# Giving VectorE 64 of the 1024 exponential units of a fused attention and spectral kernel

## The chip, the cores and the metric

The kernel runs on one core of one Trainium2 chip. The metric is device time in microseconds (us), as a median over runs. Engines of the core are called PE (TensorE: matmuls, with PEld for its weight loads), DVE (VectorE), ACT (ScalarE), POOL (GpSimd) and SP (SyncE, which here only issues DMAs). Each engine takes its own instructions in the order in which the program gives them; between engines they wait for each other by semaphores.

## The reference

Two branches are computed from one input `x` of 2048 tokens by 448 features and are mixed by a gate:

```python
x = A_x
g = _sigmoid((x * gate_w).sum(-1, keepdims=True))
a = _A_ref(x, A_wqkv, A_wo)      # softmax attention
b = _B_ref(x, B_w_r, B_w_i)      # irfft2(rfft2(x) * W)
return g * a + (1 - g) * b
```

In `_A_ref` there are 16 heads of 28 features: `q`, `k`, `v` come from `x @ wqkv`, then `p = softmax(q k^T * 28**-0.5)`, `o = p v`, and the heads together are multiplied by `wo`. The exponentials of the softmax are 16 x 2048 x 2048 values, and they are what the kernel is built around. `_B_ref` is a two-dimensional real Fourier transform, a product with a complex filter, and the transform back; the kernel does it with matmuls against constant matrices. Everything enters and leaves as bf16.

## The kernel before, in words

**Prologue.** `x` is loaded and transposed on PE, and the first keys and queries are projected. From then on the method `stream` (line 463) writes the order of PE, ACT and DVE by hand, in a loop over steps.

**Units and groups.** A group `g` is a block of 512 queries and four heads; there are 16. In a group, the 2048 keys are cut into 16 blocks `i` of 128, and each of the four heads `j` gives one *unit*: scores of 128 keys by 512 queries, which are one PSUM bank. So there are 16 x 16 x 4 = 1024 units. The four units of one `(g, i)` are a *quad*.

**A step.** [...]Five hold scores, as two slots of three and two banks (`SLOTS`), one holds the running product with `v` (`psPV`), and two rotate for everything else (`ps_bg`, line 158: the *background banks*). One step works through one slot. ACT takes the exponential of its two or three banks in one ACTIVATE (line 662) and writes bf16 into a ring of 15 places. PE meanwhile writes the scores of the next step into the other slot (`scores`, line 546, with matmuls on line 549), and multiplies a quad whose four exponentials are ready with `v` (`pv`, line 569; four matmuls on line 577). When a group's 16 quads are in, `finish_group` (line 713) copies `psPV` away and sets two later tasks going, which divide by the row sums.

**Background.** The other work is two generators of small pieces, one for the projections of attention and one for the Fourier branch. A background tile is filled by PE in one of the two banks, in two to four pieces, and emptied by DVE. `background` (line 511) gives PE pieces until their sum reaches `rate` times the index of the current unit, so they are spread evenly over the units; `st["open"]` tells that a tile is half filled. At the end, blocks of the output projection (`out_block`, line 743) join it.

**Filler.** Each step takes `HEAT` = 340 columns per unit of ACT from an account, and each background piece pays its columns in. When the account is negative, one matmul on zeros is put ahead of the scores of the next step (line 564), and 512 is paid in.

**The code that the change switches on.** `pick` (line 634) can take a quad out of the list that ACT works through (`taken`), and put its two halves, of two units each, on a list for DVE. `vscores` (line 612) gives at most one unit's score matmul per step, and only where no background tile is half filled. `vpair` (line 596) takes a background bank for it and lets DVE move the bank to an int32 tile with a clamp and an offset. When both units of the half are there, `vnext` (line 622) gives the pieces of `vexp` (line 756), which forms the exponential from integer and fraction by a polynomial, in six DVE instructions over 1024 elements. The planner gives pieces as long as its count of DVE's work, `self.dv`, is below `st["vtime"]`, which grows by 0.47 for every unit of ACT. With `VQ` = 0 the first line of `pick` always returns, and none of this is in the program.

## Time and profile before

| What | Value |
|---|---|
| Time, median of three runs | 509.69 us (509.38 to 510.75) |
| Profiled execution: its time, and the span from first to last instruction | 510.75 us, 508.9 us |
| Stretch of the exponentials in the span | 23.8 to 489.9 us |
| ACT, PE, DVE busy in that stretch of 466.1 us | 464.63, 430.47, 178.14 us |
| Granted PE clock, mean over the span | 0.983 |

Busy time is the time in which an engine runs at least one instruction that works on data; instructions of one engine can overlap, so that their durations added up are more than that. The ends of matmuls are modelled in the profile. An idle time is put down to the instruction whose semaphore came last.

### The profile page before, as it was taken

To read this page: it belongs to the slowest core of one execution; us is meant where nothing else is said; L and a number is where in the kernel's file an instruction comes from. 1 tells how busy PE (TensorE), PEld (TensorE's weight loads), DVE (VectorE), ACT (ScalarE), POOL (GpSimd) and SP (SyncE) were. 2 spreads that over 40 slices of the span, in tenths; PEclk is the share of its full clock that TensorE was granted. 3 is DMA by queue.
4 is the path that set the end of the run, shared out by engine and by line. 5 is a ranking of instruction groups with operands and counts; after the bars stand their busy time and mean duration, and the time that the engine had idled before them with its cause. 6 is when DMAs were issued, how large, how long until landed. Compare 5 with 4: busy or idle time off the path is not lost.

```text
span 508.9 us, 7848 instructions
## 1 busy us (share of the span) xinstructions
PE 453.6 (89%) x3306; PEld 159.2 (31%) x3333; DVE 195.5 (38%) x355; ACT 473.3 (93%) x426; POOL 13.8 (3%) x43
## 2 busy tenths in 40 slices
PE   6799999999999999899999999999999999998943
PEld 3433222243233333343333332233233323322211
DVE  3622323422344446645664444423344322322202
ACT  2599999999999999999999999999999999999950
POOL 7100000000000000000000000000000000000000
PEclk9999999999999999999999999999999999999986
DMA  7620000001000012312200000001001011001101
GB/s 244 145 56 9 17 7 4 21 1 30 1 23 0 20 27 51 80 44 66 52 23 13 1 22 23 32 12 34 12 20 34 15 48 32 29 27 32 36 4 55
DMA packets 28138, 17.85 MB, mean 35 GB/s; under 512 B 18568, under 2 KB 25160, under 8 KB 28104
## 3 DMA queue, kind: packets, MB, share of 16 engines
q1 hardware_dynamic: 26184, 17.06, 11.9%
q8 instruction: 26, 0.43, 0.3%
q10 hardware_dynamic: 1920, 0.30, 0.3%
q14 instruction: 8, 0.07, 0.0%
HBM read 15.25 MB, written 1.97 MB: 34 GB/s over the span
## 4 chain that ended last, share of the span: by engine, by line
ACT 85%; PE 8%; DMA 3%; DVE 2%; SPq 1%; issue 0%; ACTq 0%; DVEq 0%
ACT ring L662 85%; PE pf L748 3%; PE psS L549 2%; PE psPV L577 1%; DMA wst_65<-in_A_wqkv_dram 1%; DMA rb<-scr_639 1%; DMA wst_66<-in_A_wqkv_dram 1%; PE psS L564 1%; PE xt L319 1%; DMA rs<-oU 0%; PE pk L256 0%; DVE kT_138 L264 0%; DMA scr_639<-rc 0%; DVE kmin L276 0%; SPq L169 0%
## 5 line engine op out<-in xcount | busy, mean ns | idle before, releaser
L662 ACT ACTIVATE ring<-psS 128x1536 bf16<-128x1536 f32 (+1 forms) x410 | 464.7, 1389 | 4.1 <-PE psS L549 3.6
L577 PE MATMUL psPV<-ring,vsb 128*32 128x512 bf16 x1024 | 102.7, 389 | 0.4 <-ACT ring L662 0.3
L564 PE MATMUL psS<-zero 128*128 128x512 bf16 x219 | 82.6, 377 | 15.0 <-ACT ring L662 12.6
L549 PE MATMUL psS<-qT_136,kT_140 32*128 32x512 bf16 x256 | 40.2, 383 | 6.0 <-ACT ring L662 4.6
L549 PE MATMUL psS<-qT_134,kT_138 32*128 32x512 bf16 x256 | 40.2, 383 | 5.8 <-ACT ring L662 3.9
L577 PEld LDWEIGHTS <-vsb 128*32 128x32 bf16 x1024 | 26.5, 92 | 58.5 <-issue 58.4
L549 PE MATMUL psS<-qT_135,kT_139 32*128 32x512 bf16 x256 | 40.2, 383 | 5.0 <-ACT ring L662 3.7
L549 PE MATMUL psS<-qT_137,kT_141 32*128 32x512 bf16 x256 | 40.1, 383 | 2.0 <-ACT ring L662 1.4
L807 DVE CAST U<-psA 128x512 bf16<-128x512 f32 x32 | 22.0, 691 | 22.9 <-PE psA L803 22.9
L549 PEld LDWEIGHTS <-kT_138 32*128 32x128 bf16 x256 | 12.3, 90 | 44.0 <-issue 41.2
L549 PEld LDWEIGHTS <-kT_141 32*128 32x128 bf16 x256 | 11.4, 90 | 42.7 <-issue 41.6
L549 PEld LDWEIGHTS <-kT_140 32*128 32x128 bf16 x256 | 12.6, 90 | 38.6 <-issue 36.6
L564 PEld LDWEIGHTS <-zero 128*128 128x128 bf16 x219 | 21.4, 98 | 8.5 <-issue 7.5
L549 PEld LDWEIGHTS <-kT_139 32*128 32x128 bf16 x256 | 12.7, 90 | 35.0 <-issue 32.6
L407 DVE CAST vsb<-pvx 128x448 bf16<-128x448 f32 x16 | 10.0, 627 | 32.4 <-PE pvx L403 32.4
L886 DVE TENSOR_SCALAR bm_sb<-psY,omg 128x448 bf16<-128x448 f32 x16 | 10.9, 684 | 29.4 <-PE psY L881 29.4
L719 DVE COPY oU<-psPV 128x512 f32<-128x512 f32 x16 | 11.1, 691 | 26.0 <-PE psPV L577 25.8
L881 PE MATMUL psY<-Binv_sb,ZT 128*128 128x448 bf16 x64 | 20.6, 360 | 0.0
L751 DVE SCALAR_TENSOR_TENSOR fin<-pf,gsb,bm_sb 128x448 bf16<-128x448 f32 x16 | 10.9, 684 | 24.2 <-PE pf L748 24.2
L909 DVE CAST ZT<-psZ 128x512 bf16<-128x512 f32 x16 | 11.1, 691 | 15.9 <-PE psZ L905 15.8
L403 PEld LDWEIGHTS <-xT 128*128 128x128 bf16 x256 | 13.7, 97 | 10.9 <-issue 9.5
L748 PE MATMUL pf<-Wo_sb,qT_137 128*128 128x448 bf16 x16 | 6.5, 408 | 9.1 <-DVE qT_137 L735 9.1
(231 smaller groups left out, 425.2 us busy)
## 6 DMA issues: line engine op xcount, KB each, us to landing
RBg<-cRB SPq DMA_DIRECT2D x16, 128.0 KB, 2.8
rb<-scr_638 SPq DMA_DIRECT2D x8, 256.0 KB
rb<-scr_639 SPq DMA_DIRECT2D x8, 256.0 KB
Wg<-in_B_w_r_dram SPq DMA_DIRECT2D x32, 56.2 KB, 1.9
xtok<-in_A_x_dram SPq DMA_DIRECT2D x4, 448.0 KB, 5.7
out_dram<-fin SPq DMA_DIRECT2D x16, 112.0 KB, 1.7
CSg<-cCS SPq DMA_DIRECT2D x16, 96.0 KB, 1.9
Wg<-in_B_w_i_dram SPq DMA_DIRECT2D x16, 56.2 KB, 2.0
```

The source lines that it names most:

```text
L403: nc.tensor.matmul(pv[:, k, 0:N], lhsT=self.xT[:, c, 128 * t:128 * (t + 1)], rhs=w[:, c, 2 * n0:2 * n0 + N], start=(c == 0), stop=(c == se ...
L549: nc.tensor.matmul(ps, lhsT=self.kT[T][r:r + 32, 128 * i:128 * (i + 1)], rhs=self.qT[T][r:r + 32, QW * b:QW * (b + 1)], start=True, stop=T ...
L564: nc.tensor.matmul(psS[:, 0, :], lhsT=self.zero[:, 0:P], rhs=self.zero[:], start=True, stop=True)
L577: nc.tensor.matmul(psPV[g][r:r + 32, :], lhsT=self.vsb[:, i, 4 * T + j, :], rhs=ring[:, p, :] if isinstance(p, int) else p, start=(count[g ...
L662: ex = nc.scalar.activation(out=ring[:, rp:rp + ne, :], in_=psS[:, 0:ne, :], func=ACT.Exp, scale=self.LN)
L719: nc.vector.tensor_copy(out=oU[:], in_=psPV[:])
L748: nc.tensor.matmul(pf[:, 0:D], lhsT=self.oT[T][:, 128 * t:128 * (t + 1)], rhs=self.Wo_sb[:, T, :], start=(T == 0), stop=(T == self.NTL - 1))
L751: nc.vector.scalar_tensor_tensor(out=fin[:], in0=pf[:, 0:D], scalar=self.gsb[:, t:t + 1], in1=self.bm_sb[:, t, :], op0=ALU.mult, op1=ALU.add)
L807: nc.vector.tensor_copy(out=self.U[:, :, :, :, t * J:t * J + J].rearrange("p b r g j -> p (b r g) j"), in_=ps[:].rearrange("p b (r j) -> p ...
L881: nc.tensor.matmul(psY[:, 0:D], lhsT=Z[0:fn, fb, ri, :], rhs=self.Binv_sb[0:fn, qi, :], start=(qi == 0), stop=(qi == nq - 1))
L886: nc.vector.tensor_scalar(out=self.bm_sb[:, g, :], in0=psY[:, 0:D], scalar1=self.omg[:, g:g + 1], scalar2=None, op0=ALU.mult)
L909: nc.vector.tensor_copy(out=Zs[g][:].rearrange("p b r m -> p (b r m)"), in_=psZ[:].rearrange("p b n -> p (b n)"))
```

## The change

One constant is set: how many quads DVE takes.

```diff
@@ class Kernel @@
     RING = 15
     HEAT = 340
-    VQ = 0
+    VQ = 16
     LATE = 6
```

The line that reads it, and the one that decides whether a piece of the DVE's exponential is given now:

```python
if self.VQ * st["units"] <= len(taken) * self.NU:      # in pick; NU is 1024
    return
...
while self.dv < st["vtime"] and vnext():               # in the step
    pass
```

With 16 there is one quad for every 64 units, which is one in each group. It is taken in the first steps of the group (in the first 6 of its 16 key blocks, `LATE`), and it is the group's last key block that is not taken yet. All that follows from it, the steps of ACT, the fillers and the places of the background pieces, is laid out anew by the same planner.

## The prediction
> **What bounds the kernel now.** I read the page's busy shares first, then the windows of the stretch of exponentials, then waits, groups, and the timeline.

> ```profile
> PE 453.6 (89%) x3306; PEld 159.2 (31%) x3333; DVE 195.5 (38%) x355; ACT 473.3 (93%) x426; POOL 13.8 (3%) x43
> ...
> L662 ACT ACTIVATE ring<-psS 128x1536 bf16<-128x1536 f32 (+1 forms) x410 | 464.7, 1389 | 4.1 <-PE psS L549 3.6
> ...
> L564 PE MATMUL psS<-zero 128*128 128x512 bf16 x219 | 82.6, 377 | 15.0 <-ACT ring L662 12.6
> ```

> The exponentials keep ACT busy for 464.7 of the 466.1 us between the first and the last of them. ACT waits 3.6 us in all, 2.7 of it once, at the start. So ACT sets the end: one unit costs 464.7/1024 = 0.454 us, a step 464.7/410 = 1.13 us. Before and after lie 510.75 - 466.1 = 44.7 us (prologue, last output blocks), which the edit does not touch. But PE is close behind, and the same windows show where DVE is loaded (columns: stretch, length, busy time and count of PE, PEld, DVE, ACT, POOL, clock, DMA share, GB/s).

> ```profile
> 53.10:82.20 29.10, 26.80 (x174) 7.70 (x175) 9.97 (x19) 29.10 (x28) 0.74 (x2) 1.00 0.04 11
> ...
> 169.50:198.60 29.10, 26.99 (x206) 9.89 (x205) 14.85 (x29) 29.10 (x27) 0.53 (x1) 1.00 0.13 35
> 198.60:227.70 29.10, 26.86 (x238) 10.99 (x238) 16.38 (x36) 28.96 (x27) 0.00 (x0) 1.00 0.24 60
> 227.70:256.80 29.10, 27.00 (x215) 10.50 (x216) 16.96 (x38) 28.80 (x26) 0.00 (x0) 1.00 0.24 59
> ...
> 373.20:402.30 29.10, 27.29 (x191) 9.00 (x191) 10.48 (x18) 29.10 (x27) 0.00 (x0) 1.00 0.10 28
> ```

> A window is one group of 64 units. PE is busy for about 27 of 29.1 us in every one, DVE for 9 to 17. ACT loses time only where DVE is fullest, and the timeline shows how:

> ```profile
> 215.76 0.62 DVE L858 TENSOR_TENSOR cm_t_2359<-psB,Wg 128x450 bf16<-128x450 f32 x1
> ...
> 216.44 0.37 PE L403 MATMUL pvx<-wst_65,xT 128*128 128x112 bf16 x4 [0.72 <-DVE cm_t_2359 L858]
> ...
> 216.65 0.38 PE L564 MATMUL psS<-zero 128*128 128x512 bf16 x1
> ...
> 216.96 0.39 PE L549 MATMUL psS<-qT_135,kT_139 32*128 32x512 bf16 x2
> ...
> 217.27 0.40 PE L577 MATMUL psPV<-ring,vsb 128*32 128x512 bf16 x4
> ```

> PE wanted a background bank that DVE had not emptied, stood 0.72 us, and the scores behind it were late: ACT lost 0.14 us in that window. So a stall of PE of about 0.6 us is absorbed by the score slot already filled, and the rest is lost. The same lines price PE: from filler to scores 0.31 us, from scores to the next kind of matmul 0.31, whether scores are two or three.

> [...]the squares on 512 bf16 took 425 ns[...], the evictions of 512 f32 from PSUM 692 ns[...].[...] matmuls stay in program order; so one that waits for a bank holds the scores behind it, as above.

> **The change, part by part.**

> *Removed from ACT.* 64 units x 0.454 = 29.0 us; 410 steps become 384. ACT then needs 464.6 - 29.0 = 435.6 us.

> *PE.* 26 score turns fewer: 26 x 0.32 = -8.3 us. Each DVE unit has a score matmul of its own: 64 x 0.31 = +19.8. `pv` keeps its 1024 matmuls. The background keeps its sum and is given by unit index, so it is only denser, by 1024/960. Fillers: the account asks 340 x 64 = 21,760 columns less, and the new scores pay in 64 x 128 = 8,192 (the step adds 128 each): 29,952/512 = 58 fillers fewer, about 160 instead of 219, 58 x 0.31 = -18.0. Sum -6.5 us. PE was busy 430.5 of 466.1; it becomes 424 of 435.6, 97%. On average it fits, with 0.7 us free in a group of 27.2 us, by busy time. The true reserve is somewhat larger: matmuls with modelled ends 0.39 us after their start are followed after 0.31. This was idle 2.2 us a group before, and it is what repairs a delay.

> *DVE.* One half of a quad: two evictions 2 x 0.69 = 1.38;[...] Together 5.5 to 6.0 us; 32 halves are 176 to 193 us. I take 5.5[...].[...] With 5.5, DVE has 178 + 176 = 354 of 436 us, 81%. The planner reckons 1.3 + 0.6 + 0.95 + 0.95 + 1.15 = 4.95 a half, a tenth too little, and lets DVE's account run 0.47 per unit against ACT's 0.454; so while a half is under way DVE is given about 10 to 14% more than it can do. A half lasts some five steps, 5.6 us: it ends 0.6 to 0.8 us late, on top of a lead of one piece.

> *Where that falls.* A score for DVE takes the bank next in turn, so the following background tile gets the bank that was filled last, about 0.9 us before. Emptying it takes 0.7 us if DVE is free; every us by which DVE is late is then a us in which PE stands, with the scores behind it. In the groups with little DVE work (10 of 29.1 us) the pieces between two tiles fit and I charge only PE's crowding: two extra scores close together are 0.6 us, near what the slot absorbs; 0.25 us of ACT per group, 16 x 0.25 = 4 us. In the two groups around 198 to 257 us DVE has 16.7 + 11.0 = 27.7 us of work in 27.2: full; 0.5 us of overrun each, and some three bank waits of 0.7 us more, less what is absorbed: 2 us each, 4 us. In the three groups with 12 to 15 us: 0.5 each, 1.5 us. Sum 9.5 us of new ACT idle. No reason gives below 0; if all is absorbed it is 0. If PE's reserve is the busy figure and each of the 64 scores costs a bank wait of 0.5 us (32 us, less the 11.5 us of reserve), it is 20.

> *At nothing.* DVE's own tiles lie in SBUF and cause no DMA; the two DMAs of each group's division keep their places. A reciprocal or scaling queued behind exponential pieces on DVE comes 1 to 2 us later, and the next wants its result only groups later, except in the last group, whose quad is taken at its start and is done by its end.[...] The last exponential still leads to the same tail.

> *Sum.* Profiled execution: 510.75 - 29.0 + 9.5 = 491.2. Its time is 1.06 above the median; on the median's scale 490.

> **Rivals.** (A) Most of the gain stays, 4 to 15 us given back: 485 to 496. For it: the reserve on PE and the one-slot buffer. (B) All absorbed: 509.7 - 29 = 480.7, to 484. For it: DVE waits for PE nearly everywhere (22.9 us for one kind of tile alone), so it has air; against it: PE at 97%. (C) PE or DVE becomes the bound in most groups, 15 to 28 us given back: 496 to 508, at 500; the upper bound of bank waits above. (D) Slower: a group's quad from DVE isn't ready when its other 15 are. The group's product can't be finished, the next group's quads wait in the ring of 15 places, which fills in six steps, and then the planner drains DVE on the spot, with PE waiting for all that is left of a half, 4.1 us or more. Less the absorbed 0.6 that is 3.5 us; in all groups 56 us, time 537. It decides from 1.8 us per group. For it: in the two full groups the account leaves (0.47 x 60 = 28.2) - 17 = 11 of planned DVE work for 9.9; against it: elsewhere there is twice that. Forecast then 518. (E) The halves aren't picked, or ACT isn't relieved: same as before. Against it: the conditions of `pick` hold at each group's first step.

> **How the numbers follow.** A 0.60, B 0.15, C 0.13, D 0.09, E 0.03. Predicted 490. From 481 to 503: this leaves out D, E, a fifth of B and a third of C, about 0.19. Within 0.3% (1.5 us), which is about what a measurement can tell from no change, lies E; slower D; faster the rest, 0.88.

> **What would show it.** 384 ACTIVATEs on line 662 with about 436 us busy; idle before them some 13 us, on scores of line 549, most at 190 to 260 us; about 160 fillers;[...] DVE near 370 us on the page; PE waits on line 786, 403, 801 or 549 for DVE banks. Wrong would be made by[...] a late quad (waits of `pv` on line 577 for DVE).

## The result and the profile after

The changed kernel takes 571.23 us (median of four, 564.52 to 581.94), against 509.53 us before. The ratio is 1.116, with a 95% interval of 1.106 to 1.126: 12% slower, where 490 us and a gain of 4% were forecast. The profiled execution is the longest of the four, 581.94 us with a span of 580.2 us; it is compared with 510.75 us and 508.9 us. Executions of one kernel differ in how long the clock is low (the kernel before: 508.7 to 525.4 us at clocks of 0.990 down to 0.944), so a ratio leaves out those that lie over 1.5% above the fastest of their kernel, while medians and ranges are of all.

From the page of the changed kernel: busy times, the slices of ACT and of the granted PE clock (in tenths, 40 slices), the exponentials, the fillers, and three of the new kinds of instruction on DVE.

```profile
PE 509.1 (88%) x3282; PEld 160.1 (28%) x3310; DVE 354.0 (61%) x611; ACT 458.7 (79%) x400; POOL 14.9 (3%) x43
...
ACT  3666669899989989879889999796976668999560
...
PEclk9855559999999989869999999896985558999786
...
L662 ACT ACTIVATE ring<-psS 128x1536 bf16<-128x1536 f32 (+1 forms) x384 | 450.1, 1249 | 91.6 <-PE psS L549 88.7
...
L564 PE MATMUL psS<-zero 128*128 128x512 bf16 x196 | 83.9, 428 | 6.8 <-ACT ring L662 4.7
L601 DVE TENSOR_SCALAR zi<-psV 128x512 int32<-128x512 f32 x64 | 43.5, 680 | 12.8 <-PE psV L549 12.7
...
L775 DVE SCALAR_TENSOR_TENSOR pV<-zi,u 128x1024 uint16<-128x1024 int32 x32 | 39.1, 1222 | 0.8
```

The relief came: 384 ACTIVATEs in place of 410. But ACT now waits 91.6 us for scores, where it waited 4.1. With 450.1 us busy in place of 464.7, that is -14.6 + 87.5 = +72.9 us, which is the whole difference between the two profiled executions (71.2). The second thing to see is the clock. Before, it was 9 (full) in every slice of the stretch of exponentials but the last, which reaches beyond it. Now there are stretches of 5, and ACT falls to 6 in these.

The windows of the changed kernel show both parts (columns as in the prediction: PE, PEld, DVE, ACT, POOL busy, clock, DMA share, GB/s).

```profile
52.10:81.20 29.10, 28.03 (x105) 4.96 (x105) 12.18 (x20) 18.41 (x16) 0.00 (x0) 0.50 0.01 3
110.30:139.40 29.10, 25.77 (x205) 8.72 (x206) 19.21 (x32) 27.00 (x24) 0.28 (x1) 1.00 0.03 10
255.80:284.90 29.10, 25.79 (x227) 10.30 (x228) 24.11 (x48) 26.32 (x24) 0.00 (x0) 1.00 0.23 58
430.40:459.50 29.10, 28.63 (x130) 6.37 (x128) 11.30 (x18) 20.21 (x17) 0.00 (x0) 0.50 0.05 14
```

At half clock (0.50) PE is busy for 28.0 and 28.6 of 29.1 us and does about half as many matmuls (105 and 130, against 205 and 227), and ACT gets work for 18 to 20 us. At full clock PE is less busy than before (25.8 instead of 27 us) and ACT still lacks 2 to 3 us. In windows of 3.4 us, those with a mean clock under 0.75 add up to 153 us, with ACT busy for 63%. The other 384 us have ACT at 91.6%. Before, it was 99.7% and no window was under 0.75. So 153 x (0.997 - 0.631) = 56 us of ACT's time are lost in windows of half clock, and 384 x (0.997 - 0.916) = 31 us at full clock. The four executions differ in the same way: 564.5 us at a mean clock of 0.915, 569.9 at 0.894, 572.6 at 0.886, 581.9 at 0.856. That is 17.4 us for 0.059 of clock; carried on in a straight line to the 0.983 of before, an estimate, the clock by itself is worth some 37 us of the longest execution. By this estimate the rest of the 56 us would have been lost at full clock too.

How a low stretch begins is to be seen in the timeline of the changed kernel (start, length, engine, line, instruction; in brackets the idle time before it and what ended it).

```profile
424.06 0.69 DVE L761 TENSOR_SCALAR fr<-zi 128x1024 f16<-128x1024 uint16 x1
...
424.68 0.55 PE L881 MATMUL psY<-Binv_sb,ZT 128*128 128x448 bf16 x2
424.79 0.43 DVE L766 TENSOR_SCALAR u<-fr 128x1024 f16<-128x1024 f16 x1
...
425.13 0.68 DVE L768 TENSOR_TENSOR s<-fr 128x1024 f16<-128x1024 f16 x1
...
425.85 0.43 DVE L771 TENSOR_SCALAR s<-s 128x1024 f16<-128x1024 f16 x1
425.94 0.39 PE L549 MATMUL psV<-qT_137,kT_141 32*128 32x512 bf16 x1
426.31 0.69 DVE L772 TENSOR_TENSOR u<-s,u 128x1024 f16<-128x1024 f16 x1
427.04 1.22 DVE L775 SCALAR_TENSOR_TENSOR pV<-zi,u 128x1024 uint16<-128x1024 int32 x1
428.18 0.68 DVE L886 TENSOR_SCALAR bm_sb<-psY,omg 128x448 bf16<-128x448 f32 x1
...
428.91 0.27 PE L904 MATMUL psZ<-RBg,UT_147 128*128 128x256 bf16 x1 [2.59 <-DVE bm_sb L886]
...
429.97 1.02 ACT L662 ACTIVATE ring<-psS 128x1024 bf16<-128x1024 f32 x1 [2.48 <-PE psS L549]
```

DVE does the six instructions of one half in one run of over 4 us. PE puts a score for DVE into a background bank (425.94). The next background tile needs the bank filled just before (by line 881 at 424.68), and the eviction of that bank (line 886) stands behind the run. PE stands 2.59 us, with the next scores behind it, and ACT waits 2.48 us. The clock of these windows follows:

```profile
423.40:426.80 3.40, 2.88 (x21) 0.90 (x19) 3.26 (x7) 3.40 (x4) 0.00 (x0) 1.00 0.07 16
426.80:430.20 3.40, 1.29 (x9) 0.40 (x8) 2.62 (x4) 0.92 (x2) 0.00 (x0) 0.91 0.17 66
430.20:433.60 3.40, 3.40 (x18) 0.73 (x14) 1.29 (x2) 2.41 (x3) 0.00 (x0) 0.50 0.14 39
```

It stays at half for 54.6 us. All waits of PE for DVE, without the last one before the final output blocks, came to about 7 us before, and to about 40 us now.

Not all of the low time begins like this. The longest low stretch, from 23.41 to 84.85 us, is 61 of the 153 us and holds some 21 of the 56 us lost (ACT is busy for 65% of it). It begins before the first polynomial instruction on DVE, which starts at 28.95 us. PE's standstill just ahead of it, 1.03 us for `qT_134` of line 296, is in the kernel before as well (1.0 us). So for this stretch a run on DVE isn't shown as what set it off. Six others lie in the stretch of exponentials. Four of them follow a standstill of PE behind a whole run of the six instructions (it ends at 371.65, 394.85, 428.91 and 542.65 us), one behind three of them with a scaling and an eviction (209.41), and one behind evictions and a scaling that came right after a run (241.83).

In the traces of the two kernels, before and after, the clock is either 1.00 or 0.50, and each stretch between two changes is a whole number of 3.41 us long, from one (211.15 to 214.56 us in the changed kernel) to 140 (14.34 to 492.20 us before). Windows laid on this grid, in the changed kernel:

```profile
20.00:23.41 3.41, 2.20 (x20) 0.79 (x17) 2.31 (x6) 1.76 (x2) 0.03 (x1) 1.00 0.57 132
23.41:84.85 61.44, 58.60 (x259) 13.23 (x261) 25.45 (x43) 40.04 (x33) 0.94 (x2) 0.50 0.09 23
...
276.01:279.43 3.42, 2.69 (x22) 0.91 (x19) 3.38 (x8) 3.42 (x4) 0.00 (x0) 1.00 0.25 62
279.43:282.84 3.41, 2.19 (x20) 0.91 (x20) 2.80 (x8) 2.12 (x3) 0.00 (x0) 1.00 0.37 92
...
426.19:429.60 3.41, 0.82 (x6) 0.38 (x5) 3.20 (x5) 1.31 (x1) 0.00 (x0) 1.00 0.21 77
429.60:484.21 54.61, 53.83 (x236) 12.10 (x235) 27.78 (x44) 35.76 (x30) 0.00 (x0) 0.50 0.07 19
```

The 2.59 us of standstill at 428.91 lie in one window, and the clock falls at its end. The 1.82 us ahead of 280.65 are shared by two, and it stays.

### The profile page after: what moved, and what is told of

Its sections match the earlier page's. It is cut to its first block, busy times and chain, and to the rows that moved or that the text cites. A ratio compares the mean times of both kernels' runs of the same rounds, so it can differ in the third digit from the quotient of the medians.

```text
span 580.2 us, 8025 instructions
## 1 busy us (share of the span) xinstructions
PE 509.1 (88%) x3282; PEld 160.1 (28%) x3310; DVE 354.0 (61%) x611; ACT 458.7 (79%) x400; POOL 14.9 (3%) x43
## 4 chain that ended last, share of the span: by engine, by line
PE 42%; DVE 33%; ACT 17%; DMA 4%; issue 3%; ACTq 1%; DVEq 0%
ACT ring L662 17%; PE psS L549 12%; PE psPV L577 9%; PE psS L564 4%; DVE pV L775 4%; DVE zi L601 4%; DVE fr L761 3%; DVE s L768 3%; DVE u L772 3%; DMA rb<-scr_659 3%; PE psY L881 2%; PE pf L748 2%; PE pq L256 2%; DVE U L807 2%; DVE u L766 2%
## 5 line engine op out<-in xcount | busy, mean ns | idle before, releaser
L662 ACT ACTIVATE ring<-psS 128x1536 bf16<-128x1536 f32 (+1 forms) x384 | 450.1, 1249 | 91.6 <-PE psS L549 88.7
L577 PE MATMUL psPV<-ring,vsb 128*32 128x512 bf16 x960 | 107.0, 434 | 0.8 <-ACT ring L662 0.8
L564 PE MATMUL psS<-zero 128*128 128x512 bf16 x196 | 83.9, 428 | 6.8 <-ACT ring L662 4.7
L601 DVE TENSOR_SCALAR zi<-psV 128x512 int32<-128x512 f32 x64 | 43.5, 680 | 12.8 <-PE psV L549 12.7
L577 PEld LDWEIGHTS <-vsb 128*32 128x32 bf16 x1024 | 26.9, 94 | 78.6 <-issue 77.0
L549 PE MATMUL psS<-qT_134,kT_138 32*128 32x512 bf16 x240 | 44.4, 457 | 3.0 <-DVE qT_134 L296 1.0
L549 PE MATMUL psS<-qT_137,kT_141 32*128 32x512 bf16 x240 | 44.5, 459 | 1.0 <-issue 0.5
L549 PE MATMUL psS<-qT_136,kT_140 32*128 32x512 bf16 x240 | 38.9, 400 | 1.8 <-ACT ring L662 1.2
L549 PE MATMUL psS<-qT_135,kT_139 32*128 32x512 bf16 x240 | 39.2, 402 | 1.1 <-ACT ring L662 0.7
L775 DVE SCALAR_TENSOR_TENSOR pV<-zi,u 128x1024 uint16<-128x1024 int32 x32 | 39.1, 1222 | 0.8
L881 PE MATMUL psY<-Binv_sb,ZT 128*128 128x448 bf16 x64 | 24.6, 434 | 2.3 <-DVE zi L601 1.3
L549 PEld LDWEIGHTS <-kT_138 32*128 32x128 bf16 x256 | 11.2, 93 | 49.7 <-issue 47.6
L549 PEld LDWEIGHTS <-kT_141 32*128 32x128 bf16 x256 | 10.5, 93 | 47.2 <-issue 46.7
L564 PEld LDWEIGHTS <-zero 128*128 128x128 bf16 x196 | 20.1, 102 | 11.2 <-issue 10.5
L772 DVE TENSOR_TENSOR u<-s,u 128x1024 f16<-128x1024 f16 x32 | 22.2, 692 | 1.1
L761 DVE TENSOR_SCALAR fr<-zi 128x1024 f16<-128x1024 uint16 x32 | 22.0, 687 | 0.3
L768 DVE TENSOR_TENSOR s<-fr 128x1024 f16<-128x1024 f16 x32 | 21.9, 684 | 0.0
L549 PEld LDWEIGHTS <-kT_140 32*128 32x128 bf16 x256 | 11.1, 91 | 38.5 <-issue 36.9
```

Of the source, the lines that this page charges most:

```text
L549: nc.tensor.matmul(ps, lhsT=self.kT[T][r:r + 32, 128 * i:128 * (i + 1)], rhs=self.qT[T][r:r + 32, QW * b:QW * (b + 1)], start=True, stop=T ...
L564: nc.tensor.matmul(psS[:, 0, :], lhsT=self.zero[:, 0:P], rhs=self.zero[:], start=True, stop=True)
L577: nc.tensor.matmul(psPV[g][r:r + 32, :], lhsT=self.vsb[:, i, 4 * T + j, :], rhs=ring[:, p, :] if isinstance(p, int) else p, start=(count[g ...
L601: nc.vector.tensor_scalar(out=zi[:, QW * e:QW * (e + 1)], in0=ps[:], scalar1=self.FLOOR, scalar2=self.BIAS, op0=ALU.max, op1=ALU.add)
L662: ex = nc.scalar.activation(out=ring[:, rp:rp + ne, :], in_=psS[:, 0:ne, :], func=ACT.Exp, scale=self.LN)
L761: V.tensor_scalar(out=fr[:], in0=zi[:].bitcast(U16).rearrange("p (n two) -> p n two", two=2)[:, :, 0], scalar1=1.0 / self.ONE, scalar2=-0. ...
```

## The experiments

Each kernel was run several times beside the kernel before on the same chip; ratios are to that, and where there is none, the range is given. Theory D, later narrowed to Q: DVE comes late, PE stands at a bank behind it, and the standstill lowers the clock. Rivals: the fewer fillers let the clock fall (F); the extra scores and their banks cost it (B); the product of DVE's quad waits (W).

### Parts of the change alone

Three kernels keep the planner's order and leave out parts of the new work, so that their output is not the reference's in the taken quads. The first is the relief of ScalarE alone:

```diff
-                ps = self.ps_bg([P, QW], F32, name="psV")
-                scores(ps[:], g, i, 2 * h + e)
-                nc.vector.tensor_scalar(out=zi[...], in0=ps[:], ...)
...
-            yield from self.vexp(zi, out[:])
+            (products read self.zero; the pieces stay in the planner's account)
```

> Left out: the 64 units taken from ScalarE get neither scores nor exponentials; their four products per group read a tile of zeros. So ScalarE is relieved of 64 units, fillers are 196 as in the changed kernel, and VectorE and the background banks are as before the change. Theory D (VectorE is late, holds PE at banks and at products, and these standstills lower the PE clock): 480 to 485 us, PE clock 0.97 or more, ScalarE idle in its stretch under 10 us. Theory F (23 fillers fewer than before let the PE clock fall, whatever VectorE does): over 520 us, clock under 0.93. Theory B (the 64 extra scores and their banks cost it): 480 to 485 us as well.

Measured: 486.55 us, ratio 0.949 (0.942 to 0.956).

The second keeps scores and evictions and leaves out `vexp`:

> Left out: the six instructions of the polynomial in each of the 32 halves; the products read zeros in their place. The 64 scores, their background banks and their evictions to int32 stay. Theory D: the banks are emptied in time, 483 to 493 us, clock 0.97 or more. Theory B: near the changed kernel, over 540 us. Theory F: over 520 us.

Measured: 504.79 us, ratio 0.983 (0.974 to 0.992).

The third keeps `vexp`, on a resident tile, and leaves out scores and evictions:

```diff
-            yield from self.vexp(zi, out[:])
+            yield from self.vexp(self.zc, out[:])
```

> Left out: the 64 scores and their evictions; the polynomial runs at its places on a resident tile of zeros, so its 32 x 4.2 us on VectorE and the waits of the products for it stay, without the extra use of banks. Theory D: most of the loss stays, 525 to 565 us, clock 0.88 to 0.95, waits of PE for VectorE of 1 us and more. Theory B: 480 to 490 us. Theory F: as e1_act_only, over 520 us.

Measured: 518.71 us, ratio 1.011 (1.002 to 1.020).

The exponentials in the pages of the three, in this order (count, busy us, mean ns, idle before us):

```profile
L659 ACT ACTIVATE ring<-psS 128x1536 bf16<-128x1536 f32 (+1 forms) x384 | 436.6, 1308 | 5.6 <-PE psS L549 4.9
```

```profile
L664 ACT ACTIVATE ring<-psS 128x1536 bf16<-128x1536 f32 (+1 forms) x384 | 440.1, 1280 | 17.6 <-PE psS L549 16.4
```

```profile
L659 ACT ACTIVATE ring<-psS 128x1536 bf16<-128x1536 f32 (+1 forms) x384 | 440.9, 1272 | 31.0 <-PE psS L551 30.0
```

With ACT's relief alone the prediction's base is there: 436.6 us busy (435.6 forecast), 5.6 us idle, and the clock stays full in the profiled execution although there are 23 fillers fewer than before. That rules out the fewer fillers as the cause by themselves (theory F). The other two lie between the forecasts: the scores alone cost more than theory D allowed (483 to 493) and far less than B (over 540), the polynomial alone less than D allowed (525 to 565) and more than B (480 to 490). The 64 scores and evictions cost 504.8 - 486.6 = 18 us, the polynomial 518.7 - 486.6 = 32 us; both together, in the changed kernel, 571.2 - 486.6 = 85. Some 35 us come only when the two meet (these are medians of four, and single executions of the three spread by 10 to 24 us). That a run on DVE costs most where a score has just taken the spare bank fits this, but isn't shown by it.

### More fillers

```diff
-    HEAT = 340
+    HEAT = 400
```

> The whole change, with HEAT 400 in place of 340: 275 fillers in place of 196, all computed. Theory D: the standstills of PE stay, the clock falls less often; 79 x 0.31 = 24 us more PE work; 520 to 560 us, clock 0.92 to 0.98. Theory F: the clock is back at 0.98 and the time under 500 us.

Measured: 579.33 us (567.36 to 579.91), clock 0.90 to 0.92. That is slower than either theory forecast. Fillers don't help: they stand in PE's queue with its other work, and in the trace of the changed kernel none ran in the 2.59 us of standstill that end at 428.91.

### Which standstill

The product of the quad from DVE, later:

```diff
-                quads.append(((g, i), st["cur"] + 2))
+                quads.append(((g, i), st["cur"] + 6))
```

> The whole change, but a quad that VectorE has computed goes to its product six steps after its last piece was given, not two. Theory W (the wait of the product for the last exponential is the main standstill of PE): the 5.6 us of such waits go, and with them the long cold stretches of PE; 510 to 530 us, clock over 0.95. Theory Q (PE stands at background banks, whose eviction is queued behind a run of exponential pieces on VectorE): 555 to 570 us, clock under 0.92.

Measured: 581.87 us (562.59 to 593.45). The 5.6 us of waits of the product are gone from the profile, but the low stretches aren't; theory W falls.

The planner's account of DVE corrected to what the trace shows:

```diff
-            st["vtime"] += 0.47 * ne
+            st["vtime"] += 0.42 * ne
-            st["vtime"] = max(min(st["vtime"], self.dv + 1.0), self.dv - 3.0)
+            st["vtime"] = max(min(st["vtime"], self.dv + 0.3), self.dv - 3.0)
```

(with 0.72, 0.72, 1.15, 1.15 and 1.25 for the eviction and the pieces)

> The whole change, with the planner's account of VectorE set to the durations measured: 0.72 for an eviction, 0.72, 1.15, 1.15 and 1.25 for the four pieces, 0.42 instead of 0.47 for a unit of ScalarE, and a lead of at most 0.3 instead of 1.0. Theory Q: fewer pieces in one run, PE stands less, 520 to 545 us, clock 0.93 to 0.97. Theory W: little changes as the product still comes two steps after the last piece, 555 to 570 us.

Measured: 549.04 us, ratio 1.058 (1.045 to 1.070). Better, but slower than forecast: DVE's quads now come so late that the product waits for them (PE for the last exponential 8.2 us, for the copy of a group's product 12.4 us), as in the prediction's rival D.

At most one piece in a step, with a later product, and the output blocks of a group four steps later:

```diff
-            while self.dv < st["vtime"] and vnext():
-                pass
+            if self.dv < st["vtime"]:
+                vnext()
...
+        later.append((s + 14, outs))
```

> The whole change, with at most one exponential piece for VectorE in a step, the product six steps after the last piece, and the output blocks of a group four steps later, so that they don't meet a scaling that is still queued. Theory Q: no standstill of PE over 1.5 us, clock 0.96 or more, 505 to 525 us: near e2_scores_only with 504.8, as PE's own work is then the bound. Rival (VectorE is simply full): over 540 us.

Measured: 522.90 us, ratio 1.024 (1.017 to 1.030), clock 0.94. Most of the loss is gone with the same instructions, but the clock is lower than forecast. In one place PE still stood 1.18 us at a bank behind a piece, a score and a scaling, and a low stretch of 34 us followed.

The same with fewer fillers (`HEAT` 290):

> As e7_one_piece, with HEAT 290 in place of 340: 104 fillers instead of 196, 92 x 0.31 = 28 us less PE work. If PE's own work is the bound once its standstills are gone, 485 to 500 us with the clock at 0.96 or more. If the fillers are what holds the clock, it falls under 0.90 and the time is over 540 us.

Measured: 529.12 us, ratio 1.027 (1.018 to 1.036), clock 0.86 to 0.93. Neither forecast holds: 28 us less PE work gains nothing, and the clock falls a little, not under 0.90 in most runs. PE's own work isn't the bound here.

A step's rest for the banks after a score for DVE (output blocks wait likewise):

```diff
             if st["open"] is None and vscores():
                 cols += 128
+                wake[0] = max(wake[0], s + 1)
+                wake[1] = max(wake[1], s + 1)
```

> As e7_one_piece, and in a step in which a score for VectorE has taken a background bank no new background tile is begun, so that the bank filled before it has a step more to be emptied. Theory Q (what is left in e7_one_piece is PE standing at the bank filled last): standstills of PE behind VectorE under 10 us besides the last one, clock 0.97 or more, 495 to 508 us. If PE's own work is the bound instead: 515 to 525 us as e7_one_piece.

Measured: 524.96 us, ratio 1.028 (1.024 to 1.032). A miss: no gain on e7_one_piece. Perhaps the work that is put off crowds the next step; that isn't shown.

The same rest in the unaltered change:

> The whole change with only that step's rest for the banks after a score for VectorE. Theory Q with long runs of pieces as the larger part: 540 to 565 us, clock 0.90 to 0.94. If the neighbouring bank is the larger part: 505 to 525 us.

Measured: 553.50 us, ratio 1.076 (1.072 to 1.080): as forecast for long runs as the larger part; the neighbouring bank is the smaller one. (The fillers come to 210 here, not 196.)

Half the units, in the manner of e9_one_piece_bank:

> As e9_one_piece_bank with VQ 8: VectorE takes 32 units instead of 64. ScalarE is relieved of 14.5 us. Theory Q: half of the extra waits, 497 to 508 us, clock 0.97 or more.

Measured: 518.78 us, ratio 1.018 (1.013 to 1.023). Worse than forecast: the loss doesn't shrink with the gain.

### A run on VectorE by itself

In the kernel before, with all units on ScalarE, the six instructions on a resident tile, 16 times, result unused:

```diff
+            if st["units"] // 64 >= bursts:
+                bursts += 1
+                for _ in self.vexp(self.zc, spare[:]):
+                    pass
             cols += background(1200)
```

> The kernel before (ScalarE does all 1024 units), all computed, with a run of the six polynomial instructions on a resident tile of zeros once in each group: 16 runs of 4.2 us on VectorE whose result is not used. It has no scores for VectorE, no relief of ScalarE and no wait of a product. If a run on VectorE by itself is hidden by VectorE's idle time: 510 to 513 us. Theory Q: PE stands up to 2 us in some of the 16 groups; without an effect on the clock that is under 16 x 1.5 = 24 us, 512 to 534 us with the clock at 0.98; if the standstills also set the clock back, 515 to 560 us with the clock at 0.90 to 0.97 and whole stretches at half.

Measured: 602.16 us (589.30 to 614.05), clock 0.80 to 0.86: 16 x 4.14 = 66 us of DVE work, on an engine that is busy for 38%, cost 92 us, more than theory Q forecast. The waits of PE in its profile (us, times, longest):

```profile
PE psPV L579 <- DVE oU L727: 17.5, 7, 3.3
...
PE pn L294 <- DVE U L815: 3.2, 1, 3.2
PE psB L858 <- DVE UT L830: 2.4, 1, 2.4
PE pk L258 <- DVE X_sb L798: 2.4, 1, 2.4
```

and its windows around one of them:

```profile
85.60:89.00 3.40, 3.09 (x24) 0.98 (x23) 2.16 (x5) 3.40 (x4) 0.00 (x0) 1.00 0.00 0
89.00:92.40 3.40, 1.34 (x10) 0.42 (x11) 3.30 (x6) 3.05 (x3) 0.00 (x0) 0.93 0.02 2
92.40:95.80 3.40, 2.88 (x11) 0.45 (x10) 1.23 (x3) 1.27 (x1) 0.00 (x0) 0.50 0.02 2
```

Again PE stands (busy for 1.34 of 3.40 us), and then the clock is at half (0.50), in a kernel without any of the change's scores. But the placing was unlucky: the run came ahead of the copy that frees the one bank of a group's product, which the changed kernel's runs don't. So the same 96 instructions were put in the middle of each group, one per step, and then in one run:

```diff
+            if st["units"] >= 64 * bursts + 16:
+                bursts += 1
+                chain = self.vexp(self.zc, spare[:])
+            if chain is not None and next(chain, 0) == 0:
+                chain = None
...  (in vexp, a yield between the two instructions of the second and third piece)
```

> The kernel before with all 1024 units on ScalarE, and 16 times the six polynomial instructions on a resident tile of zeros, result unused, one instruction in a step, from the 16th unit of each group on. Theory Q: hidden, 509 to 515 us, clock 0.97 or more. If the amount counts: like e16_burst_mid.

Measured: 512.64 us, ratio 1.003 (1.002 to 1.005).

> The same 96 instructions as in e14_spread, from the same unit of each group, but each six in one run of 4.2 us; away from the copy of the group's product. Theory Q: PE stands 1 to 2.5 us in most groups, the clock falls after some of them: 525 to 580 us, clock 0.85 to 0.95. If runs cost only ahead of that copy: 509 to 515 us.

Measured: 515.09 us, ratio 1.009 (1.006 to 1.012), clock 0.98. Less than theory Q forecast. There, a run finds the two banks alone with the background, and PE's longest standstill behind one is 1.5 us. So what a run costs is set by what is queued behind it, and a group's only product bank is the dear place. That a bank next to a score is another is argued from the 35 us above; `e3_chain_only` has no such scores and still loses 32 us, with twice as many runs as here.

### One instruction in a step

```diff
-            while self.dv < st["vtime"] and vnext():
-                pass
+            if self.dv < st["vtime"]:
+                vnext()
...  (in vexp, between the two instructions of the second and third piece)
+        yield
```

> The whole change, with at most one polynomial instruction for VectorE in a step, and nothing else. If runs of pieces are what loses the time: 503 to 515 us, near e13_one_op with 506.3. If the late product or the early output blocks carry a large part: 520 us or more.

Measured: 516.03 us (507.24 to 522.47), ratio 1.002 (0.999 to 1.006), clock 0.973 in the profiled execution. With the same instructions on every engine and the same 196 fillers, only the places of DVE's instructions in its queue, and what follows from them, are changed, and 571.2 - 516.0 = 55 of the 62 us are gone.

With the product four steps after the last instruction, and the later output blocks of e7_one_piece:

> As e7_one_piece, with the two pieces of two instructions cut in two, so that VectorE gets at most one polynomial instruction (0.42 to 1.22 us) in a step, and the product four steps after the last one. Theory Q: no run left, standstills of PE behind VectorE under 15 us besides the last, clock 0.97 or more, 500 to 512 us. If the amount of VectorE's work is the cause: 515 us or more, as e7_one_piece.

Measured: 506.33 us, ratio 0.990 (0.983 to 0.996). This beats both kernels, by 1% on the one before. In its page the clock is low only at the start, and ACT still waits 28.7 us:

```profile
PEclk9955999999999999999999999999999999999996
...
L662 ACT ACTIVATE ring<-psS 128x1536 bf16<-128x1536 f32 (+1 forms) x384 | 443.0, 1273 | 28.7 <-PE psS L549 27.2
```

Half the units in this manner:

> As e13_one_op with 32 units instead of 64. Theory Q: ScalarE's relief of 14.5 us less some 8 us for the scores and waits: 500 to 508 us.

Measured: 517.96 us (508.63 to 538.59 over twenty runs), ratio 1.005 (1.001 to 1.009), at clocks from 0.976 down to 0.904. A miss; why half the units do worse than all isn't settled.

No quad for DVE in the first group:

```diff
-            if self.VQ * st["units"] <= len(taken) * self.NU:
+            if st["units"] < 64 or self.VQ * st["units"] <= (len(taken) + 1) * self.NU:
```

> As e13_one_op, with no quad for VectorE in the first group: 60 units instead of 64. If the cold stretch of PE at the start comes from the first quad on top of the prologue: 492 to 503 us, clock 0.98. If it falls as it likes: 500 to 512 us.

Measured: 510.91 us (503.73 to 526.71), ratio 0.992 (0.989 to 0.996), as in the second forecast. The clock isn't held by this: the profiled execution has no low stretch at the start, but a slice of 6 and one of 7 elsewhere. Whether the first quad sets off the stretch at the start stays open; in `e13_one_op`, as in the changed kernel, the clock falls (at 24.1 us) before the first polynomial instruction (29.5 us).

## Why the prediction was wrong

- **Base and prices held.** ACT's relief alone gives 486.6 us, with 436.6 us busy against 435.6 forecast. The 5.5 us taken for a half were the author's estimate: of its parts, the trace of the kernel before shows only the evictions. In the changed kernel the six instructions took 0.69, 0.43, 0.69, 0.42, 0.69 and 1.22 us and the evictions 0.68: 5.5 us a half. The 0.69 of the first is for 1024 elements that are every second 16-bit word.
- **The step that failed first is "Where that falls": 9.5 us of new ACT idle.** It was 87.5. The prediction let a half's pieces last "some five steps" and end 0.6 to 0.8 us late. The trace has 14 of the 32 halves back to back, 4.2 us in one run, and one to six other instructions within each of the other 18. The loop gives pieces until the account is level, with no eviction between them, and a waiting eviction is queued behind. So the lateness at a bank is up to the whole run, 2.6 us at 428.9, not 0.7. e17_one_op_only breaks up every run (the shortest half takes 4.9 us, with seven instructions in its span) and takes back 55 us.
- **The missing term is the clock.** The prediction had full clock throughout, and read the 1.00 of every window as a given. 56 of the 87 us were lost in windows of half clock (0.50), some 37 of them by the estimate above through the clock itself. Standstills of PE of 1.12 to 2.92 us came ahead of six of the low stretches.
- **"A stall of about 0.6 us is absorbed, the rest is lost"** was right in kind, not in size: 2.59 us of standstill at 428.9 gave 2.48 us of ACT idle, so 0.11 was absorbed. What it left out is that a late PE has only 2 to 3% of free time to catch up, by the prediction's own 97%, and almost none at half clock (28.63 of 29.10 us busy).
- **"At nothing" was wrong in one place.** A scaling that comes late was to be wanted "only groups later". In the last four groups the output blocks want it at once: at 542.7 us PE had stood 2.92 us for it behind a run, and the clock fell again.
- **Fillers:** 196, not about 160. The account is capped at 1024 columns, so that credit is lost where background comes in bursts; that this is the whole difference follows from the code alone and wasn't measured. The effect is small (e4_heat, e8_less_filler).
- **Busy ACT:** 450.1 us in place of 435.6. One by one after waits, a pair of ACTIVATEs took 2.47 us, where back to back before it took 2.30 (last section).
- **Rival D** was the right side with the wrong mechanism: waits of the product for DVE were 5.6 us, and taking them away gained nothing (e5_late_product). Its 0.09 was too little: ACT at 99.7% and PE at 92% with in-order queues is a balance with two ways to tip, and the prediction priced only the gentle one.

What stays open: what sets off the low stretch at the start, and when a low stretch ends. Those in the changed kernel's stretch of exponentials last from 3.4 to 61 us; in the two longest PE is busy for 58.6 of 61.4 and 53.8 of 54.6 us. The last section has a measure that goes with the clock in the two traces, but no run here varied it by itself.

## What to carry to other kernels

Work moved to an idle engine isn't hidden by its idle time, but by the gaps between the instructions that others wait for: give it in pieces shorter than those gaps, one at a time (516.0 us here, against 571.2 in runs). Price a standstill of PE not by its length alone: look whether the granted clock falls after it (to 0.50 for 54.6 us after the 2.59 us at 428.91; not after the 1.82 us ahead of 280.65). When two engines are both above 90% busy, ask first how a delay on a third reaches them, and then what the relief is worth.

## What the runs showed of the hardware

| Such columns in a window | Windows at full clock, and how many of them half clock followed | Windows at half clock, and how many of them full clock followed |
|---|---|---|
| under 2300 | 9, all 9 | 8, none |
| 2300 to 3500 | 19, 3 | 45, 9 |
| 3500 and over | 234, none | 1, the one |

- The windows of the kernel before hold 3072 to 5632 such columns in the stretch of exponentials, half of them over 4484. The windows at half clock in the changed kernel hold 1280 to 3392 in its stretch of exponentials up to 549.1 us, half of them under 2913. That the clock follows from these sums isn't shown.
- Ten exponentials of 1536 and 1024 columns in turn, back to back in the kernel before (from 99.70 us), take 11.49 us, 2.30 a pair; one by one after waits, a pair takes 1.45 + 1.02 = 2.47 us.
